# The last routing of a layer in two halves, behind given products, and VectorE in emission order in one step

## The chip, the cores and the metric

One core of one Trainium2 chip runs the whole kernel. The metric is the device time of one execution in microseconds. A profiled execution has a span as well, from its first to its last instruction.

## What is computed

An attention with decay (no softmax), then two layers of experts. Cut to what matters:

```
scores = q k^T / 8;  x = (scores * decay) v            # 4 x 8 heads, 576 x 64  ->  2304 tokens x 512
# layer 1: capacity 576 per expert
e = argmax(x w_gate);  g = softmax(x w_gate)[e]
x = g * (relu(x w1[e]) w2[e])                           # 512 -> 1024 -> 512, 8 experts
# layer 2: only tokens with x . w_skip > 0, no capacity
e = argmax(x w_gate2); g = softmax(x w_gate2)[e]
out = x + g * (relu(x w1b[e]) w2b[e])                   # skipped tokens: out = x
```

## The kernel before

The kernel is one program in a language whose planner decides the order of instructions on each engine. It places them by their order of emission and its own estimate of when their inputs are ready; a block may ask that some engines keep the order of emission (`manual_schedule`). The experts run under such a block for GpSimd (`Pool`) alone. So TensorE's, VectorE's and ScalarE's orders are the planner's, and what is emitted later can be placed earlier when it seems ready.

**Layers, steps and f.** Each layer is run as nine steps (`NST`; `pos` in the code), each with a batch of up to `CAPS[layer][pos]` tokens of one expert. In layer 2 step 0 has 240 columns, step 1 has 324 and step 2 has 240. A step runs over f = 0 to 7, blocks of 128 of the 1024 hidden units (`Layer.run`, L800). For each f there is a first product h (`s1`, L712, its matmuls in L727 or L732 to L734) and a second product y (`s2`, L740, in L755 to L757, L763 or L766 to L768). Where a step has more than 192 columns, the weights and inputs are split into a high and a low part, and each product takes three matmuls. ScalarE makes the high half `hi` (L673) and VectorE subtracts for the low half `lo` (L674), one unit (two f) ahead; h gives `hh` on ScalarE (L737) and `hl` on VectorE (L738). Step 0 of layer 2 is one of the steps in which y has tokens on its rows (`token_major`, L770); there h is emitted one f further ahead.

**Hand-over from step to step.** While a step runs, the rows of the next are gathered by an indirect transfer on GpSimd (`gather`, L683 and L838; its index is `fx` for the first steps and `gix` for the others), transposed on TensorE (`transposes`, L704: `x_1T` is that of step 1), and written as `x_1h` by ScalarE (L705) and `x_1l` by VectorE (L707). At the end of a step of layer 1, `post1` (L874) computes layer 2's logits for its tokens (`M`, `Mt`, `L`), transposes the result back to rows (`yr`, L797), writes it to memory for layer 2 and to the output, and routes the tokens: `Router.add` (L386).

**Routing.** `Router.add` is a generator that stops at its `yield`s. It takes the largest logit (`mx`, `oh`), the softmax's probability (`gt`, L331: a subtraction on GpSimd, an exponential on ScalarE, the rest on VectorE), counts per expert (`cum`, `C`), then on TensorE the ranks (`R`, L418 and L419), from them on VectorE the slot of every token (`lo`, `hi`, `A`, `k3`), products with what is to be stored per slot (`vv`, L458, and `B`, L460: token numbers and the gate in two parts), and a matmul `I` (L466) that is added to the table `inv` (L468). In names, `s8` is the routing after the last step of layer 1 and `r3` the last routing before layer 1. After the last routing `order` (L515; `fc` is its count on TensorE) sorts the experts by count, `by_order` (L530; `w` and `invp`, L538 and L540) brings a table's values into that order, `int_idx` (L590) makes the gather's index and `scatter_idx` (L579; `sif`, `six`) that of the output. `leave` (L545; names `lv2...`) and `left_out` (L959) count the tokens that found no place, for a fallback at the end.

**Where it stands before.** In layer 1's first step the routing `r3` goes on in hooks behind f = 0 and 2, and order, gates and indices follow behind f = 4 (L942). The last routing `s8` runs through to `I` in `post1`, in front of layer 2's first step, with `order` between its parts; then come `by_order([0])` and the gather's index, and in step 0 of layer 2 the gates behind f = 1 (`gates2`). The gather of step 1 is emitted at f = 0, its transposes at f = 6. `leave2` is emitted behind step 1; as its inputs are ready long before, the planner can place it earlier.

Of the kernel before, what the change touches and what calls it, by code (L numbers as in the profile page):

```python
# [11 lines left out]
F32R = mybir.dt.float32r  # L12
# [11 lines left out]
KT = 3  # L24
# [7 lines left out]
NST = 9  # L32
# [297 lines left out]

def softmax_top(g, L, T, t_, oh):  # L331

    nc = g.nc
    v_ = nc.vector
    b = [128, T, 8]
    l8 = L[:, :, 0:8]
    mx = t_("mx", [128, T])
    v_.tensor_reduce(out=mx, in_=l8, op=ALU.max, axis=AX.X)
    first_max(g, oh, l8, mx, t_("e8", b), t_("mn", [128, T]), T)
# [27 lines left out]
class Router:  # L367
# [15 lines left out]
    def ohf(g_, t0, T):  # L383
        return g_.oh[:, t0:t0 + T].bitcast(F32)

    def add(g_, t0, T, L, vals, name, late=False, mid=False):  # L386
        g, lay, nv = g_.g, g_.lay, g_.nv
        nc = g.nc
        v_ = nc.vector
# [4 lines left out]
        b = [128, T, 8]  # L394
        oh, ohf = g_.oh[:, t0:t0 + T], g_.ohf(t0, T)
        if lay == 1:
            gt = softmax_top(g, L, T, t_, oh)
            cm = None
        else:
            o1 = t_("o1", b)  # L400
            cm = t_("cm", [128, T])
            v_.tensor_single_scalar(cm, L[:, :, 8], 0.0, op=ALU.is_gt)
            gt = softmax_top(g, L, T, t_, o1)
            v_.tensor_mul(oh, o1, cm[:, :, None].to_broadcast(b))
        if late:
            s8, sh = t_("s8", b), t_("shf", [128, T])
            v_.tensor_mul(s8, ohf, g_.shift.to_broadcast(b))
            v_.tensor_reduce(out=sh, in_=s8, op=ALU.add, axis=AX.X)
# [40 lines left out]
                                in1=g.k128[:, None, :].to_broadcast([128, T, KT]), op0=ALU.mult, op1=ALU.is_equal)  # L449
        vt = t_("vt", [128, T, nv], F32R)  # L450
        vtf = vt.bitcast(F32)
        for i, x in enumerate(vals):
            nc.gpsimd.tensor_copy(vt[:, :, i], x)
        v_.tensor_copy(vt[:, :, nv - 2], gt)
        v_.tensor_sub(vt[:, :, nv - 1], gt, vtf[:, :, nv - 2])
        nc.gpsimd.tensor_copy(g_.gt[:, t0:t0 + T], gt)
        vv = t_("vv", [128, T, nv, 8])
        v_.tensor_mul(vv, v[:, :, None, :].to_broadcast([128, T, nv, 8]), vtf[:, :, :, None].to_broadcast([128, T, nv, 8]))  # L458
        Bm = t_("B", [128, T, nv * 8, KT], F32R)
        v_.tensor_mul(Bm, vv.rearrange("p t i e -> p t (i e)")[:, :, :, None].to_broadcast([128, T, nv * 8, KT]),  # L460
                      k3[:, :, None, :].to_broadcast([128, T, nv * 8, KT]))
        yield cm
        I = misc(g, f"{name}I")
        w = nv * NTAU
        for t in range(T):
            nc.tensor.matmul(I[:, 0:w], A[:, t, :], Bm[:, t].rearrange("p a k -> p (a k)"), start=(t == 0), stop=(t == T - 1))  # L466
        inv = g_.inv.rearrange("p i e k -> p (i e k)")
        v_.tensor_add(inv, inv, I[:, 0:w])  # L468

    def counts(g_, name):  # L470
        g = g_.g
# [125 lines left out]
def tokens_out(g, b):  # L597

    nc = g.nc
    n0 = 9 * (b // 2) + (4 if b % 2 else 0)  # L600
    T = 5 if b % 2 else 4
    s = K()

    def logits():
        s.l4 = g.rt1.tile([128, 640], F32, tag="l4", name=f"l4_{b}", bufs=1)
        logits4(g, g.xT[b], g.wg1, [512] if T == 4 else [320, 320], s.l4, f"L4_{b}_")

    def choose():
        L = g.rt1.tile([128, T, NL], F32, tag="L1", name=f"L1_{b}")
        token_logits(g, s.l4, T, L, f"Lt{b}_")  # L610
        s.gen = g.r1.add(n0, T, L, [g.tid1[:, n0:n0 + T]], f"r{b}", late=b > 1, mid=b == 1)
# [65 lines left out]
class Layer:  # L677
# [62 lines left out]
    def s2(self, pos, f):  # L740
# [7 lines left out]
        if self.token_major(pos):  # L748
            for k in range(TILES[2][pos]):
                n = min(128, C - 128 * k)  # L750
                y, ks = s.y[k][0:n], slice(128 * k, 128 * k + n)
                if C <= F32_MAX:
                    nc.tensor.matmul(y, s.hh[f][:, ks], w.r2[:, f % 2], start=a, stop=o)
                else:
                    nc.tensor.matmul(y, s.hh[f][:, ks], w.hi2[:, f % 2], start=a, stop=False)  # L755
                    nc.tensor.matmul(y, s.hh[f][:, ks], w.lo2[:, f % 2], start=False, stop=False)  # L756
                    nc.tensor.matmul(y, s.hl[f][:, ks], w.hi2[:, f % 2], start=False, stop=o)  # L757
            return
        for d in range(4):
            dc = slice(128 * d, 128 * d + 128)  # L760
            y = s.y[d][:, 0:C]
            if C <= F32_MAX:
                nc.tensor.matmul(y, w.r2[:, f % 2, dc], s.hh[f], start=a, stop=o)  # L763
            else:
                wh, wl = w.hi2[:, f % 2, dc], w.lo2[:, f % 2, dc]
                nc.tensor.matmul(y, wh, s.hh[f], start=a, stop=False)  # L766
                nc.tensor.matmul(y, wh, s.hl[f], start=False, stop=False)  # L767
                nc.tensor.matmul(y, wl, s.hh[f], start=False, stop=o)  # L768

    def token_major(self, pos):  # L770

# [26 lines left out]
        return n, ps  # L798

    def run(self, hooks, inner={}):  # L800
        g, lay = self.g, self.lay
        base = 4 * NST * (lay - 1)
        for pos in range(NST):
            for f in range(8):
                u = base + 4 * pos + f // 2
                if f % 2 == 0:
# [13 lines left out]
                for i in range(f + 1, f + 2 + self.token_major(pos)):  # L820
                    if i < 8:
                        self.s1(pos, i)
                    elif nx is not None:
                        nx.s1(np_, i - 8)
                self.s2(pos, f)
                if (pos, f) in inner:
                    inner[pos, f]()
            self.evac(pos)
            self.post(pos)
            if pos in hooks:  # L830
                hooks[pos]()


def gather_rows(g, src, idx, C, name, lim=None):
# [18 lines left out]
def moe(g):  # L853
# [20 lines left out]
    def post1(pos):  # L874
# [11 lines left out]
        for k in range(T):  # L886
# [6 lines left out]
        for i, cm in enumerate(r2.add(t0, T, L, [g.slot[:, t0:t0 + T], sl(r1.invp, pos, 0)], f"s{pos}", late=pos == NST - 1)):  # L893
            if i == 0 and pos == NST - 1:
                r2.order()
# [13 lines left out]
    def post2(pos):  # L909
        s = l2.st[pos]  # L910
        for k in range(TILES[2][pos]):
            n, ps = l2.rows(pos, k)
            o = g.rt.tile([128, 512], F32, tag="xr", name=f"o{pos}_{k}", bufs=6)
            v_.scalar_tensor_tensor(out=o[0:n], in0=ps[0:n], scalar=col(r2.gate, 2, pos, k, n), in1=s.rows[k][0:n], op0=ALU.mult, op1=ALU.add)  # L914
            scatter(g, col(g.si2, 2, pos, k, n), o[0:n])

    idx20 = []
# [28 lines left out]


def keep_gates(g):
# [321 lines left out]
```

## Time and profile before

| | us |
|---|---|
| median of 3 runs | 584.06 (583.22 to 586.92) |
| profiled execution | 584.51 |
| its span | 582.6 |
| TensorE busy in the span | 550.9 |
| VectorE busy | 309.7 |
| ScalarE busy | 226.3 |
| GpSimd busy | 144.8 |

Attention lasts up to about 113 us, layer 1 up to about 374, layer 2 to the end. The busy time of TensorE is that of pipelined matmuls: neighbours overlap, and the distance of two starts is what one costs. The mean granted clock of TensorE in the span is 0.982 of full speed.

### The profile page before, as it was taken

The numbers are of one execution on the slowest core, as the hardware profiler recorded it, in microseconds if no ns is written. First come the engines' busy times: TensorE is split into PE (matmuls) and PEld (weight loads), VectorE is DVE, ScalarE is ACT, GpSimd is POOL, SyncE is SP. The second block draws the span as 40 slices with busy tenths as digits, with TensorE's granted clock in tenths as the row PEclk, the third lists the DMA queues.
The fourth block names the chain that finished last, engine by engine and source line by source line (L and its number), as shares of the span: only waits on it lengthen the run. The fifth ranks groups of instructions, "written<-read, shape, count | busy, mean of one in ns | idle before, by whom it ended". The sixth has DMA issues, their size and how long they took to land.

```text
span 582.6 us, 12184 instructions
## 1 busy us (share of the span) xinstructions
PE 550.9 (95%) x4545; PEld 513.8 (88%) x4545; DVE 309.7 (53%) x926; ACT 226.3 (39%) x457; POOL 144.8 (25%) x192
## 2 busy tenths in 40 slices
PE   5999989999899999999999999879999999999991
PEld 5989879788899999999999999768998999999980
DVE  4767889445365756767676767695556201110110
ACT  2343444413444545455455555534443222112110
POOL 4355362012221140405040304050204112210110
PEclk7899999999999999999999999989999999999997
DMA  8869786187875474655465556367646378788860
GB/s 193 188 177 252 200 252 241 42 270 224 285 258 195 155 244 156 206 176 187 162 215 154 187 169 206 123 199 232 220 129 204 131 247 257 224 278 262 259 210 9
DMA packets 116085, 116.20 MB, mean 199 GB/s; under 512 B 47654, under 2 KB 88870, under 8 KB 116018
## 3 DMA queue, kind: packets, MB, share of 16 engines
q1 hardware_dynamic: 104432, 90.12, 50.8%
q0 software_dynamic: 6320, 15.74, 8.4%
q10 hardware_dynamic: 5266, 9.48, 4.4%
q8 instruction: 38, 0.62, 0.4%
q14 instruction: 29, 0.24, 0.1%
HBM read 101.11 MB, written 17.92 MB: 204 GB/s over the span
## 4 chain that ended last, share of the span: by engine, by line
PE 81%; DVE 8%; DMA 5%; SPq 1%; issue 1%; POOL 1%; ACT 1%; POOLq 0%; DVEq 0%
PE h L727 10%; PE y L763 9%; PE h L732 6%; PE h L734 6%; PE h L733 6%; PE y L767 6%; PE y L768 5%; PE y L766 5%; PE S L187 3%; PE O L229 3%; PE O L223 2%; PE yr L797 2%; PE y L755 1%; PE Tk L170 1%; PE y L756 1%; PE y L757 1%
## 5 line engine op out<-in xcount | busy, mean ns | idle before, releaser
L674 DVE TENSOR_TENSOR lo<-r,hi 128x1024 fp32r<-128x1024 f32 x80 | 97.9, 1224 | 65.2 <-ACT hi L673 63.3
L673 ACT CAST hi<-r 128x1024 fp32r<-128x1024 f32 x80 | 83.9, 1049 | 66.2 <-PE y L767 28.3
L767 PE MATMUL y<-hl,hi 128*128 128x316 f32 (+7 forms) x256 | 76.4, 300 | 0.9 <-DVE hl L738 0.8
L768 PE MATMUL y<-hh,lo 128*128 128x316 f32 (+7 forms) x256 | 75.9, 298 | 0.0
L766 PE MATMUL y<-hh,hi 128*128 128x316 f32 (+7 forms) x256 | 73.3, 298 | 0.0
L763 PE MATMUL y<-hh,r 128*128 128x168 f32 (+3 forms) x448 | 71.6, 302 | 1.6 <-ACT hh L729 1.6
L763 PEld LDWEIGHTS y<-hh,r 128*128 128x128 f32 x448 | 64.6, 190 | 2.0 <-ACT hh L729 1.8
L737 ACT ACTIVATE hh<-h 128x240 fp32r<-128x240 f32 (+8 forms) x80 | 32.1, 401 | 71.9 <-PE h L734 70.1
L785 DVE COPY yt<-y 128x168 f32<-128x168 f32 (+11 forms) x30 | 11.8, 395 | 89.0 <-ACT yt L787 64.4
L729 ACT ACTIVATE hh<-h 128x168 f32<-128x168 f32 (+4 forms) x64 | 19.3, 302 | 95.7 <-PE h L727 95.4
L845 POOL DMA_INDIRECT out<-o,six x18 | 19.2, 1065 | 144.7 <-DVE o L914 142.6
L738 DVE SCALAR_TENSOR_TENSOR hl<-h,hh 128x240 fp32r<-128x240 f32 (+8 forms) x80 | 35.4, 443 | 31.6 <-ACT hh L737 31.6
L767 PEld LDWEIGHTS y<-hl,hi 128*128 128x128 f32 x256 | 48.2, 188 | 2.1 <-DVE hl L738 1.9
L768 PEld LDWEIGHTS y<-hh,lo 128*128 128x128 f32 x256 | 48.2, 188 | 0.0
L766 PEld LDWEIGHTS y<-hh,hi 128*128 128x128 f32 x256 | 47.1, 188 | 0.1
L845 POOL DMA_INDIRECT out<-x2r,si x24 | 27.8, 1158 | 10.4 <-issue 6.0
L190 DVE TENSOR_TENSOR P<-S,tab 128x512 f32<-128x512 f32 (+1 forms) x40 | 23.7, 631 | 11.2 <-PE S L187 10.9
L838 POOL DMA_INDIRECT g<-xd,gix x20 | 23.9, 1194 | 9.4 <-issue 5.8
L154 POOL TENSOR_TENSOR vh<-v,tab 128x512 f32<-128x512 f32 x15 | 16.2, 1082 | 26.3 <-PE O L229 17.2
L207 DVE TENSOR_TENSOR st<-st,kv 64x64 f32<-64x64 f32 x96 | 20.9, 218 | 3.0
L797 PE MATMUL yr<-ident,yt 128*128 128x128 f32 (+11 forms) x148 | 21.9, 280 | 0.5 <-DVE o L914 0.5
L187 PE MATMUL S<-qT,kT 64*128 64x128 f32 x288 | 22.4, 295 | 0.0
(757 smaller groups left out, 1288.4 us busy)
## 6 DMA issues: line engine op xcount, KB each, us to landing
r<-w1a SPq DMA_DIRECT2D x36, 512.0 KB, 4.8
r<-w2a SPq DMA_DIRECT2D x36, 512.0 KB, 4.0
r<-w1b SPq DMA_DIRECT2D x36, 512.0 KB, 5.5
r<-w2b SPq DMA_DIRECT2D x36, 512.0 KB, 4.0
xd<-xr ACTq DMA_DIRECT2D x18, 256.0 KB, 3.9
k<-k SPq DMA_DIRECT2D x32, 128.0 KB, 3.3
q<-q SPq DMA_DIRECT2D x16, 256.0 KB, 3.8
v<-v SPq DMA_DIRECT2D x32, 128.0 KB, 4.1
```

Of the source, the lines that this page charges most:

```text
L187: nc.tensor.matmul(S[hh][:, c], s.kT[hp, cs], s.qT[hp, cs], start=True, stop=True)
L673: nc.scalar.copy(hi, raw)
L674: nc.vector.tensor_sub(lo, raw, hi.bitcast(F32))
L727: nc.tensor.matmul(ps, w.r1[:, c, fc], s.xh[:, c, 0:C], start=(c == 0), stop=(c == 3))
L732: nc.tensor.matmul(ps, w.hi1[:, c, fc], s.xh[:, c, 0:C], start=(c == 0), stop=False)
L733: nc.tensor.matmul(ps, w.hi1[:, c, fc], s.xl[:, c, 0:C], start=False, stop=False)
L738: nc.vector.scalar_tensor_tensor(out=s.hl[f], in0=ps, scalar=0.0, in1=s.hh[f].bitcast(F32), op0=ALU.max, op1=ALU.subtract)
L763: nc.tensor.matmul(y, w.r2[:, f % 2, dc], s.hh[f], start=a, stop=o)
L766: nc.tensor.matmul(y, wh, s.hh[f], start=a, stop=False)
L767: nc.tensor.matmul(y, wh, s.hl[f], start=False, stop=False)
L768: nc.tensor.matmul(y, wl, s.hh[f], start=False, stop=o)
L845: r = g.nc.gpsimd.indirect_dma_start(out=g.oa["out"][:, :], out_offset=IndirectOffsetOnAxis(ap=idx, axis=0), in_=rows, in_offset=None, bou ...
```

## The change

Only the order of work changes, and which engine does one subtraction. In the last routing of each layer (`last`) `Router.add` is cut into more parts. First come ranks, slots and the product for the token numbers, then their `I`; later come the softmax's probability (its subtraction now on VectorE), the product for the two gate values and a second `I`. Hooks place the parts behind given f of the next layer's first step, and each hook runs in `issue_after(mm)`: TensorE's instructions in it stay behind the last y matmul of that f. In that step the gather for step 1 is emitted at f = 3 in both layers, and its transposes and step 1's first h at f = 7. Step 0 of layer 2 is emitted in a block that keeps VectorE in order of emission; what is emitted outside it may still be placed among its instructions. The left-over count is held behind the last row product of step 1 on VectorE.

```diff
 def softmax_top(g, L, T, t_, oh):
+    return probability(g, L, T, t_, top(g, L, T, t_, oh))
...
+def probability(g, L, T, t_, mx, last=False):
...
-    nc.gpsimd.tensor_sub(sh, l8, mx[:, :, None].to_broadcast(b))
+    (v_ if last else nc.gpsimd).tensor_sub(sh, l8, mx[:, :, None].to_broadcast(b))
...
+        def gates():
+            v_.tensor_copy(vt[:, :, nv - 2], gt)
+            v_.tensor_sub(vt[:, :, nv - 1], gt, vtf[:, :, nv - 2])
+            nc.gpsimd.tensor_copy(g_.gt[:, t0:t0 + T], gt)
...
+        spread(0, nv - 2)
         yield cm
+        place(0, nv - 2)
+        yield cm
+        gt = probability(g, L, T, t_, mx, True)
+        gates()
+        spread(nv - 2, nv)
+        yield cm
+        place(nv - 2, nv)
...
         for pos in range(NST):
+            with ExitStack() as ctx:
+                if (self.lay, pos) == (2, 0):
+                    ctx.enter_context(self.g.tc.manual_schedule(engines={mybir.EngineType.Pool, mybir.EngineType.DVE}))
+                self.step(pos, inner)
+            self.post(pos)
...
-                    if f == (3 if (lay, pos) == (1, 0) else 0) and (nx is not self or pos == 0):
+                    if f == (3 if pos == 0 else 0) and (nx is not self or pos == 0):
                         nx.gather(np_)
...
-                        if f == 6:
+                        if f == (7 if pos == 0 else 6):
                             nx.transposes(np_)
...
-                    elif nx is not None:
+                    elif nx is not None and (pos or f == 7):
                         nx.s1(np_, i - 8)
...
+        gen = r2.add(t0, T, L, [g.slot[:, t0:t0 + T], sl(r1.invp, pos, 0)], f"s{pos}", late=last, last=last)
+        cm = next(gen)
+        if last:
+            g.step2 = lambda: next(gen, None)
...
+    def behind(fn):
+        def run(mm):
+            with g.tc.issue_after(mm):
+                fn()
+        return run
+
+    def order1():
+        r1.order()
+        r1.by_order([0])
+        g.gi1 = r1.int_idx(0)
+
     def gates1():
-        r1.order()
-        r1.by_order([0, 1, 2])
-        g.gi1 = r1.int_idx(0)
+        g.step3()
+        r1.by_order([1, 2])
         g.sf1, _ = r1.scatter_idx(0)
+    def ranks2():
+        g.step2()
+        r2.order()
+
+    def idx2():
+        g.step2()
+        r2.by_order([0])
+        g.gi2 = r2.int_idx(0)
+
+    def softmax2():
+        g.step2()
+
     def gates2():
+        g.step2()
         r2.by_order([1, 2, 3])
         _, g.si2 = r2.scatter_idx(1)
 
     def leave2():
-        r2.leave()
-        left_out(g)
+        with g.tc.issue_after(g.row):
+            r2.leave()
+            left_out(g)
...
-    l1.run({1: r1.leave, NST - 3: r2.pick_first, NST - 2: early2}, {(0, 0): g.step3, (0, 2): idx1, (0, 4): gates1})
-    r2.by_order([0])
-    g.gi2 = r2.int_idx(0)
-    l2.run({1: leave2}, {(0, 1): gates2})
+    l1.run({1: r1.leave, NST - 3: r2.pick_first, NST - 2: early2}, {(0, 0): behind(g.step3), (0, 2): behind(idx1), (0, 4): behind(order1), (0, 5): behind(g.step3), (0, 6): behind(gates1)})
+    l2.run({1: leave2}, {(0, 0): behind(ranks2), (0, 2): behind(idx2), (0, 4): behind(softmax2), (0, 5): behind(gates2)})
```

## Rows read from the trace of the kernel before

**Rows 1.** The page: busy us of TensorE, its share, instructions

```profile
PE 550.9 (95%) x4545; PEld 513.8 (88%) x4545; DVE 309.7 (53%) x926; ACT 226.3 (39%) x457; POOL 144.8 (25%) x192
```

**Rows 2.** TensorE's waits, 350 to 425 us: line <- releaser: total us, times, longest

```profile
PE s8I L466 <- DVE s8B L460: 3.0, 1, 3.0
PE fc L473 <- DVE C L414: 1.3, 1, 1.3
```

**Rows 3.** TensorE's waits, 100 to 150 us

```profile
PE x_1T L704 <- DMA g<-xd,fx: 1.7, 1, 1.7
```

**Rows 4.** Stretches: length, PE, PEld, DVE, ACT, POOL busy, PEclk, DMA share, GB/s

```profile
377.75:380.40 2.65, 1.41 (x12) 1.44 (x13) 2.07 (x17) 0.95 (x3) 0.00 (x0) 1.00 0.56 204
380.40:384.10 3.70, 0.71 (x5) 0.52 (x4) 3.70 (x20) 0.85 (x2) 2.19 (x3) 0.94 0.15 33
384.10:387.60 3.50, 3.50 (x14) 3.07 (x14) 3.33 (x16) 0.37 (x1) 1.12 (x2) 0.57 1.00 336
387.60:409.20 21.60, 21.60 (x140) 19.04 (x140) 13.76 (x27) 10.36 (x17) 6.04 (x5) 1.00 0.72 232
```

**Rows 5.** Timeline of layer 1's first step: start, duration (us), engine, line, operation

```profile
131.37 0.55 PE L704 MATMUL x_1T<-ident,g 128*128 128x128 f32 x3 [1.72 <-DMA g<-xd,fx]
...
133.44 1.30 PE L763 MATMUL y<-hh,r 128*128 128x168 f32 x8
...
134.58 1.30 PE L727 MATMUL h<-x_1h,r 128*128 128x168 f32 x8
```

**Rows 6.** Timeline of TensorE at the handover to layer 2

```profile
376.10 1.20 PE L797 MATMUL yr<-ident,yt 128*128 128x128 f32 x8
...
385.53 0.64 PE L755 MATMUL y<-hi,hh 128*128 128x512 f32 x1
...
387.64 0.27 PE L732 MATMUL h<-x_0h,hi 128*128 128x240 f32 x1
...
388.98 0.40 PE L755 MATMUL y<-hi,hh 128*128 128x512 f32 x1
...
390.37 0.27 PE L732 MATMUL h<-x_0h,hi 128*128 128x240 f32 x1
...
409.19 0.31 PE L766 MATMUL y<-hh,hi 128*128 128x324 f32 x1
```

**Rows 7.** Timeline of VectorE, the same stretch

```profile
378.35 0.34 DVE L564 TENSOR_REDUCE lv2cm<-oh 128x24 f32<-128x192 f32 x1
...
379.50 0.17 DVE L422 TENSOR_TENSOR s8r<-oh,s8R 128x16 f32<-128x16 f32 x1
...
388.03 0.42 DVE L538 TENSOR_TENSOR w<-inv,ord2PO 128x192 f32<-128x192 f32 x1
388.36 0.18 DVE L965 TENSOR_REDUCE lfr<-lv2left 128x1 f32<-128x24 f32 x1
...
388.88 0.18 DVE L543 TENSOR_TENSOR sgate<-invp 128x24 f32<-128x24 f32 x1
...
389.52 0.18 DVE L587 CAST six<-sif 128x24 int32<-128x24 f32 x1
390.15 1.23 DVE L674 TENSOR_TENSOR lo<-r,hi 128x1024 fp32r<-128x1024 f32 x1 [0.45 <-ACT hi L673]
391.29 0.40 DVE L738 SCALAR_TENSOR_TENSOR hl<-h,hh 128x240 fp32r<-128x240 f32 x1
391.66 1.23 DVE L674 TENSOR_TENSOR lo<-r,hi 128x1024 fp32r<-128x1024 f32 x1
...
403.74 0.89 DVE L707 TENSOR_TENSOR x_1l<-x_1T,x_1h 128x324 fp32r<-128x324 f32 x2
```

**Rows 8.** GpSimd's timeline; last, issues 370 to 420 us: count, median us to landing

```profile
386.44 1.01 POOL L838 DMA_INDIRECT g<-x2d,gix  x1 [2.23 <-DVE gix L593]
...
389.04 0.95 POOL L838 DMA_INDIRECT g<-x2d,gix  x1 [0.30 <-issue]
...
g<-x2d,gix POOLq DMA_INDIRECT x7, 6.1
```

More of the change, by code (lines that the diff above doesn't have):

```diff
@@ L331, in softmax_top, with top @@
 def softmax_top(g, L, T, t_, oh):
+    return probability(g, L, T, t_, top(g, L, T, t_, oh))
+def top(g, L, T, t_, oh):
+    l8 = L[:, :, 0:8]
+    mx = t_("mx", [128, T])
+    g.nc.vector.tensor_reduce(out=mx, in_=l8, op=ALU.max, axis=AX.X)
+    first_max(g, oh, l8, mx, t_("e8", [128, T, 8]), t_("mn", [128, T]), T)
+    return mx
+def probability(g, L, T, t_, mx, last=False):
     nc = g.nc
@@ L384, in ohf, with add @@
         return g_.oh[:, t0:t0 + T].bitcast(F32)
-    def add(g_, t0, T, L, vals, name, late=False, mid=False):
+    def add(g_, t0, T, L, vals, name, late=False, mid=False, last=False):
         g, lay, nv = g_.g, g_.lay, g_.nv
@@ L396, in add @@
         if lay == 1:
-            gt = softmax_top(g, L, T, t_, oh)
+            mx = top(g, L, T, t_, oh)
             cm = None
@@ L402, in add @@
             v_.tensor_single_scalar(cm, L[:, :, 8], 0.0, op=ALU.is_gt)
-            gt = softmax_top(g, L, T, t_, o1)
+            mx = top(g, L, T, t_, o1)
             v_.tensor_mul(oh, o1, cm[:, :, None].to_broadcast(b))
+        if not last:
+            gt = probability(g, L, T, t_, mx)
         if late:
@@ L451, in add, with spread @@
         vtf = vt.bitcast(F32)
+        vv = t_("vv", [128, T, nv, 8])
+        Bm = t_("B", [128, T, nv * 8, KT], F32R)
+        def gates():
+            v_.tensor_copy(vt[:, :, nv - 2], gt)
+            v_.tensor_sub(vt[:, :, nv - 1], gt, vtf[:, :, nv - 2])
+            nc.gpsimd.tensor_copy(g_.gt[:, t0:t0 + T], gt)
+        def spread(i0, i1):
+            n = i1 - i0
+            v_.tensor_mul(vv[:, :, i0:i1], v[:, :, None, :].to_broadcast([128, T, n, 8]), vtf[:, :, i0:i1, None].to_broadcast([128, T, n, 8]))
+            v_.tensor_mul(Bm[:, :, 8 * i0:8 * i1], vv[:, :, i0:i1].rearrange("p t i e -> p t (i e)")[:, :, :, None].to_broadcast([128, T, 8 * n, KT]),
+                          k3[:, :, None, :].to_broadcast([128, T, 8 * n, KT]))
@@ L452, in add, with place @@
+        def place(i0, i1):
+            I = misc(g, f"{name}I{i0}")
+            w = (i1 - i0) * NTAU
+            for t in range(T):
+                nc.tensor.matmul(I[:, 0:w], A[:, t, :], Bm[:, t, 8 * i0:8 * i1].rearrange("p a k -> p (a k)"), start=(t == 0), stop=(t == T - 1))
+            inv = g_.inv[:, i0:i1].rearrange("p i e k -> p (i e k)")
+            v_.tensor_add(inv, inv, I[:, 0:w])
         for i, x in enumerate(vals):
             nc.gpsimd.tensor_copy(vt[:, :, i], x)
-        v_.tensor_copy(vt[:, :, nv - 2], gt)
@@ L455, in add @@
[L455 to L461, printed above, removed]
@@ L462, in add @@
-        yield cm
[L463 to L468, printed above, removed]
+        if not last:
+            gates()
+            spread(0, nv)
+            yield cm
+            place(0, nv)
+            return
+        spread(0, nv - 2)
+        yield cm
@@ L470, in counts @@
+        place(0, nv - 2)
+        yield cm
+        gt = probability(g, L, T, t_, mx, True)
+        gates()
+        spread(nv - 2, nv)
+        yield cm
+        place(nv - 2, nv)
     def counts(g_, name):
@@ L610, in choose @@
         token_logits(g, s.l4, T, L, f"Lt{b}_")
-        s.gen = g.r1.add(n0, T, L, [g.tid1[:, n0:n0 + T]], f"r{b}", late=b > 1, mid=b == 1)
+        s.gen = g.r1.add(n0, T, L, [g.tid1[:, n0:n0 + T]], f"r{b}", late=b > 1, mid=b == 1, last=b == 3)
         next(s.gen)
@@ L752, in s2 @@
                 if C <= F32_MAX:
-                    nc.tensor.matmul(y, s.hh[f][:, ks], w.r2[:, f % 2], start=a, stop=o)
+                    self.mm = nc.tensor.matmul(y, s.hh[f][:, ks], w.r2[:, f % 2], start=a, stop=o).ins
                 else:
@@ L756, in s2 @@
                     nc.tensor.matmul(y, s.hh[f][:, ks], w.lo2[:, f % 2], start=False, stop=False)
-                    nc.tensor.matmul(y, s.hl[f][:, ks], w.hi2[:, f % 2], start=False, stop=o)
+                    self.mm = nc.tensor.matmul(y, s.hl[f][:, ks], w.hi2[:, f % 2], start=False, stop=o).ins
             return
@@ L762, in s2 @@
             if C <= F32_MAX:
-                nc.tensor.matmul(y, w.r2[:, f % 2, dc], s.hh[f], start=a, stop=o)
+                self.mm = nc.tensor.matmul(y, w.r2[:, f % 2, dc], s.hh[f], start=a, stop=o).ins
             else:
@@ L767, in s2 @@
                 nc.tensor.matmul(y, wh, s.hl[f], start=False, stop=False)
-                nc.tensor.matmul(y, wl, s.hh[f], start=False, stop=o)
+                self.mm = nc.tensor.matmul(y, wl, s.hh[f], start=False, stop=o).ins
     def token_major(self, pos):
@@ L800, in run, with step @@
     def run(self, hooks, inner={}):
-        g, lay = self.g, self.lay
-        base = 4 * NST * (lay - 1)
         for pos in range(NST):
+            with ExitStack() as ctx:
[3 more added lines that the diff above has]
+            self.post(pos)
+            if pos in hooks:
+                hooks[pos]()
+    def step(self, pos, inner):
+            g, lay = self.g, self.lay
+            base = 4 * NST * (lay - 1)
             for f in range(8):
@@ L826, in run @@
                 if (pos, f) in inner:
-                    inner[pos, f]()
+                    inner[pos, f](self.mm)
             self.evac(pos)
-            self.post(pos)
-            if pos in hooks:
-                hooks[pos]()
 def gather_rows(g, src, idx, C, name, lim=None):
@@ L892, in post1 @@
             xs.append((n, xr))
-        for i, cm in enumerate(r2.add(t0, T, L, [g.slot[:, t0:t0 + T], sl(r1.invp, pos, 0)], f"s{pos}", late=pos == NST - 1)):
-            if i == 0 and pos == NST - 1:
-                r2.order()
+        last = pos == NST - 1
+        gen = r2.add(t0, T, L, [g.slot[:, t0:t0 + T], sl(r1.invp, pos, 0)], f"s{pos}", late=last, last=last)
+        cm = next(gen)
+        if last:
+            g.step2 = lambda: next(gen, None)
+        else:
+            for _ in gen:
+                pass
         f = g.rt.tile([128, KT], F32, tag="sf", name=f"sf{pos}")
@@ L913, in post2 @@
             o = g.rt.tile([128, 512], F32, tag="xr", name=f"o{pos}_{k}", bufs=6)
-            v_.scalar_tensor_tensor(out=o[0:n], in0=ps[0:n], scalar=col(r2.gate, 2, pos, k, n), in1=s.rows[k][0:n], op0=ALU.mult, op1=ALU.add)
+            g.row = v_.scalar_tensor_tensor(out=o[0:n], in0=ps[0:n], scalar=col(r2.gate, 2, pos, k, n), in1=s.rows[k][0:n], op0=ALU.mult, op1=ALU.add).ins
             scatter(g, col(g.si2, 2, pos, k, n), o[0:n])
```

3 lines of the change are left out of this document (removed).

## The prediction

> **What bounds the kernel now.** The first view is the busy time of the engines: TensorE is busy for 95% of the span [rows 1], so a change can only win what TensorE loses, and what matters is where that is. The second view is therefore TensorE's waits, stretch by stretch. Where layer 1 hands over to layer 2 there are two: 3.0 us at the last routing's matmul `s8I` for the VectorE product `s8B`, and 1.3 us at the count `fc` for VectorE's `C` [rows 2]. In layer 1's first step there is one of 1.7 us, the transposes `x_1T` for a gather [rows 3]. The third view, busy time and granted clock by stretch, shows what the first two waits really cost: TensorE works 1.41 of 2.65 us and 0.71 of 3.70 us, and then 3.5 us pass at a granted clock of 0.57, which is close to the lower of its two levels, 1.2 GHz [rows 4]. The row of a y matmul lasts 0.64 us there (385.53) and 0.40 later (388.98) [rows 6]. After 387.6 TensorE is never idle up to 409.2 [rows 4]. So the loss sits in two places, and the change works on both.
>
> **What TensorE could gain at the handover.** I count the work from the transposes `yr` (376.10, done about 377.05 [rows 6]) to the first y matmul of step 1 of layer 2 (409.19 [rows 6]). Twelve h matmuls of step 0 take 1.34 us (387.64 to 388.98), six y matmuls 1.39 (388.98 to 390.37) [rows 6]. Still to do at 377.05: 20 h matmuls (2.2), y of f=0 (1.4), ranks and count (0.3, an estimate), h of f=3 to 7 (6.7), y of f=1 to 7 (9.7), 12 transposes `x_1T` (1.3, at 0.11 each like the h matmuls), the `I` matmuls (0.6), and 24 h matmuls of step 1 at 0.15 (3.6; its tiles are 324 columns against 240). That is 25.8 us, so 402.9. TensorE is there at 409.2: 6.3 us is the most that this place can give.
>
> **Layer 1's first step.** The transposes `x_1T` are emitted at f=7 instead of 6. Then h of f=7 and y of f=6 run first, 1.14 us per eight matmuls (133.44 to 134.58 [rows 5]), 2.3 us together. The gather that they wait for lets them go on at 131.37 [rows 5]; its index is made at the same place as before, so its landing does not move. The wait of 1.7 us is covered. The gates, which now come at f=5 and 6, are needed only after y of f=7, some 2 us after I expect them. I take 1.7; bounds 0.5 (the copies of `x_1T` are waited for instead) and 1.7.
>
> **The handover, part by part.** Three edits free VectorE. The left-over count, 13 instructions from `lv2cm` at 378.35 to `lfr` at 388.36 [rows 7], goes behind step 1: about 3 us of VectorE in the worst stretch. The product `s8B` is halved, and the softmax leaves the stretch. And the rank matmuls `s8R` and the count `fc` go behind y of f=0, so TensorE no longer stands at 377.75. The price: TensorE reaches `s8R` at 377.05 + 2.2 + 1.4 + 0.3 = 381.0, while VectorE read it at 379.50 before [rows 7]. Everything that follows on VectorE starts 1.5 us later.
>
> **VectorE in program order.** This is the edit that I cost in full, because what waits on VectorE now holds up all that was emitted behind it: weights' low halves (`lo`), which h and y of later f need, and the products `hl`. A `lo` holds VectorE for 1.14 us and an `hl` for 0.37 (starts at 390.15, 391.29, 391.66 [rows 7]). A chain of dependent small instructions goes at 0.21 (`sgate` to `six`, three steps in 0.64 [rows 7]); two chains mixed go closer. From 381.05:
> ranks (10) and order (8) at 0.21, plus 0.2 for the wide `A`: 4.0, with `hl` of f=3 done at 385.5. `lo` of the next unit 386.65 and 387.8. TensorE meanwhile has h of f=3, y of f=1 and 2 and `I`, to 385.4, then y of f=3: hardly a wait, because given products lie in front. `hl` of f=4 must wait for its h, which had to wait for `lo`: VectorE idles 1.0 and ends at 389.25. The index: inverse add 0.28, one `w` with its reduction 0.85 (388.03 to 388.88 [rows 7]), cast 0.2: the gather of step 1 is issued about 390.8, against 386.44 before [rows 8]. It is three tiles, 1.3 apart (386.44 to 389.04 [rows 8]), and lands 6.1 later (median [rows 8]): 399.5. Then `hl` of f=5, two `lo` (393.25), 1.0 idle again, `hl` of f=6 (394.7), the softmax and the second product (8 at 0.21, and 0.5 for the exponential on ScalarE: 396.9), `hl` of f=7 (397.3), which TensorE's last y needs: it is done at 398.7. Behind that on VectorE stand the gates (0.28 + 3 x 0.85 + 4 x 0.21 = 3.7: 401.1), two `lo` (403.4) and only then the four subtractions `x_1l` at 0.45 (0.89 for two [rows 7]): 405.3. Step 1's h matmuls need these. So TensorE has nothing but `x_1T` from 398.7 to about 404, and ends h of f=0 and 1 of step 1 at about 407.5: 1.7 us ahead of 409.2.
>
> That idle stretch looks like the one before the half clock [rows 4]. Half clock for about 3 us costs 1.5 more, and the gain would be 0.2. I take 0.8 between them, for the transposes still break the idle time. Bounds: +6.3 (TensorE never waits) and -2.7 (five handovers of 0.6 more from TensorE to VectorE, and the half clock).
>
> A rule of the Trainium skill bears on the price of program order (VectorE: DVE Perf Modes, The DRAIN you can't avoid): a VectorE instruction does not start before the pipe of the one before it is empty, with or without a wait between them. The rows don't bear that out fully: `lfr` starts at 388.36 while `w`, from 388.03, lasts 0.42 [rows 7]. By the rule mixing two chains wins nothing, so program order costs nothing; that is rival four.
>
> **Smaller parts.** The subtraction for the softmax moves from GpSimd to VectorE: one step of 0.21, counted above; GpSimd's scatters of x2r, which stood behind it and the gate copy, go earlier, and nothing waits for them. The gather of step 2 stands on GpSimd behind the gate copy: about 397, landing about 405, needed only during step 1. SP reads the order of experts after the order is made, at about 385, and starts the weights of step 1 then; VectorE converts them only after 401. The left-over count lies behind step 1's rows, where VectorE converts for step 2: about 4 us of small instructions among waits of the same size. I take a loss of 0.3; bounds 0 and 2.
>
> **The sum.** The profiled execution took 584.51 (span 582.6): 584.5 - 1.7 - 0.8 + 0.3 = 582.3. The median of the runs is 0.45 below that execution, so 581.9.
>
> **The rivals.**
> One, TensorE never waits: VectorE's idle times are filled and `x_1l` comes in time. For it: TensorE's demand is 25.8 us, VectorE's from 381.05 only about 22 without its waits. Against: these 22 us alone end at 403. 584.5 - 6.3 - 1.7 = 576.5, as a median 576.1; it covers 576 to 580 as waits remain.
> Two, slower: VectorE's fixed order holds `x_1l` back so long that the wait moves into step 1. Place: the gates and two `lo` ahead of `x_1l`. Price: 2.7 at the handover, 2 at the count, half of the layer 1 gain: 584.5 + 4.7 - 0.9 = 588.3, as a median 587.9. It decides if the last `x_1l` ends after about 408. For it: VectorE is full from 381 on. Against: each price is at its bound.
> Three, the stall only changes place: half clock in front of step 1, the transposes of layer 1 wait for their copies: 584.5 - 0.2 - 0.5 + 0.3 = 584.1, as a median 583.7.
> Four, program order is free: 26 small instructions at 0.17 instead of 0.21 save 1.0: 581.3, as a median 580.9. The steps from `sgate` to `six` speak against it.
>
> **How the numbers follow.** Likeliest 0.45 (581.9, its own range 580 to 584), one 0.20, two 0.13, three 0.15, four 0.07. A measurement here tells about 1% from no change, 5.8 us. Faster by more than that is below 578.2: the better part of rival one, 0.13. Slower is above 589.9: the far end of rival two, 0.05. The rest, 0.82, is within 1%. The range leaves out half of rival one below and half of rival two above: 578.0 to 586.5.
>
> **What would show it.** Right: no wait at `s8I` or `fc`; `x_1T` of layer 1 without its 1.7; VectorE busy almost throughout from 381 to 405; TensorE idle just before `x_1l`, in front of step 1 of layer 2, and a clock below 1 behind it; the gather of step 1 issued some 4 us later. Wrong: TensorE busy throughout that stretch (rival one); a wait for `I` in spite of the products in front; waits of TensorE after step 1 for `lo` or `hl`, which I have only at 0.3.

## The result: slower by 0.7%, most of it by a term sized at 0.3 us

The changed kernel takes 588.81 us (median of 11 runs, 587.0 to 590.4); the kernel before takes 584.31 beside it (11 runs). The ratio is 1.0074, with a 95% interval of 1.0057 to 1.0091. The forecast was 581.9 with a range up to 586.5. The time went up by 4.5 us, where a small gain was forecast.

The profiled execution took 589.9 us (span 587.8, before 582.6). On the page TensorE's row, which answers to [rows 1], says little: 3.7 us more busy time, with only seven more matmul rows (the second `r3I` and the second `s8I`). The stretches below show that most of this is time at a lower clock; the rest of the longer span is idle time.

```profile
PE 554.6 (94%) x4552; PEld 516.9 (88%) x4552; DVE 313.4 (53%) x934; ACT 226.8 (39%) x457; POOL 143.5 (24%) x190
```

TensorE's waits in the changed kernel (line <- releaser: total us, times, longest), from 350 to 425 us, which answers to [rows 2], and from 425 to 470:

```profile
PE h L767 <- DVE lo L707: 2.7, 2, 1.9
PE x_1T L737 <- DVE x_1l L740: 2.2, 1, 2.2
...
PE lfp L1033 <- DVE lfr L1031: 3.9, 1, 3.9
PE yr L830 <- DVE o L958: 0.5, 1, 0.5
```

The waits at `s8I`, `fc` and layer 1's `x_1T` [rows 2, 3] are gone, as the change wants it. Three others stand there now: h waits for weights' low halves, the last transposes `x_1T` wait for an `x_1l` that is late, and the left-over count's matmul `lfp` waits 3.9 us for its input. That one is the largest, and it lies in a stretch where the kernel before waits only 0.5 us. The stretches of the changed kernel show what follows each wait (columns as in [rows 4]):

```profile
381.60:383.60 2.00, 0.11 (x2) 0.08 (x1) 1.96 (x5) 0.43 (x1) 0.00 (x0) 1.00 0.00 0
383.60:387.30 3.70, 3.70 (x15) 3.26 (x16) 1.41 (x2) 0.37 (x1) 0.00 (x0) 0.54 0.88 293
...
399.30:403.40 4.10, 1.87 (x9) 1.12 (x8) 3.93 (x10) 1.48 (x3) 0.00 (x0) 1.00 0.23 65
403.40:407.40 4.00, 4.00 (x19) 4.00 (x20) 3.77 (x6) 0.86 (x2) 2.05 (x2) 0.61 0.86 311
...
440.04:443.93 3.89, 0.00 (x1) 0.03 (x1) 3.61 (x12) 0.91 (x2) 3.05 (x3) 1.00 0.60 214
443.93:449.00 5.07, 5.07 (x25) 4.41 (x26) 1.93 (x6) 0.37 (x1) 1.78 (x1) 0.66 0.75 251
```

Each time TensorE is idle for some 2 to 4 us, and after it the granted clock is 0.54, 0.61 and 0.66 for 3.7, 4.0 and 5.1 us, that is, at or near the lower of the two levels (1.2 GHz) for most of it. Had that work run at full clock, it would have taken 3.70 x 0.46 = 1.7, 4.00 x 0.39 = 1.6 and 5.07 x 0.34 = 1.7 us less (an estimate from these rows). So each of these waits cost 1.6 to 1.7 us on top of its own length.

**Where the time went.** I took three stretches out of each trace: layer 1's first step (from y of f = 0 to the first `M`), the handover (from the first `M` of layer 1's last step to the first y of layer 2's step 1, `408.91` in the changed kernel, 409.19 before [rows 6]), and the count's stretch (from the first `yr` of step 1 to the last `x_8T`). Everything behind it lasts the same to 0.1 us in the traces compared.

| kernel (one execution each, us) | layer 1's first step | handover | count's stretch | median us, ratio to the kernel before, 95% |
|---|---|---|---|---|
| before | 22.01 | 34.50 | 111.90 | 584.31 |
| changed | 20.75 | 37.26 | 117.41 | 588.81, 1.0074 (1.0057 to 1.0091) |
| e1 layer 1's edits only | 20.75 | 35.23 | 111.90 | 582.83, 0.9961 (0.9941 to 0.9982) |
| e2 count not held back | 20.75 | 39.62 | 111.90 | 587.89, 1.0049 (1.0032 to 1.0065) |
| e3 VectorE free | 20.75 | 33.74 | 118.40 | 587.54, 1.0034 (1.0010 to 1.0057) |
| e4 held count only | 22.42 | 33.68 | 118.15 | 589.66, 1.0074 (1.0048 to 1.0101) |
| e5 `lfp` later | 21.87 | 37.12 | 113.14 | 587.00, 1.0016 (0.9994 to 1.0039) |
| e6 `lfp` later, VectorE free | 21.87 | 33.98 | 113.12 | 584.60, 0.9982 (0.9964 to 0.9999) |
| e7 `lfp` later, layer 2 whole and free | 21.86 | 33.73 | 113.12 | 584.36, 0.9978 (0.9958 to 0.9998) |
| e8 e5 with the ranking later | 21.86 | 38.93 | 113.14 | 590.25, 1.0076 (1.0049 to 1.0103) |
| e9 e6 with the count at step 3 | 20.75 | 33.08 | 111.67 | 579.22, 0.9911 (0.9888 to 0.9934) |
| e10 e9 with the slots sooner | 20.75 | 30.55 | 111.66 | 577.83, 0.9886 (0.9871 to 0.9902) |
| e11 e7 with VectorE in order | 20.75 | 38.68 | 113.14 | 586.59, 1.0037 (1.0024 to 1.0050) |
| e12 e9, `lfp` placed by the planner | 20.75 | 32.13 | 112.25 | 581.15, 0.9947 (0.9926 to 0.9968) |

Ratios are against runs of the kernel before on the same chip: 584.8 for e1 to e4, 585.4 for e5 to e8, 584.3 for e9 to e11, 583.9 for e12. For the changed kernel the three stretches sum to -1.26 + 2.76 + 5.51 = +7.0 us; its span grew by 5.2, because two waits that differ from execution to execution (a y of layer 1 for `hh`, and `x_0T` for its gather) were 1.8 us shorter in this one (1.6 and 0.9 before, 0.7 and none here). The medians, 4.5 apart, hold more of that spread than one trace can show. The stretches spread too: with the same code there, the handover took 34.50 us in the kernel before and 35.23 in e1, and 32.13 to 33.98 in e3, e6, e9 and e12.

### The profile page after: what moved, and what is told of

Its sections match the earlier page's. It is cut to its first block, busy times and chain, and to the rows that moved or that the text cites. A ratio compares the mean times of both kernels' runs of the same rounds, so it can differ in the third digit from the quotient of the medians.

```text
span 587.8 us, 12204 instructions
## 1 busy us (share of the span) xinstructions
PE 554.6 (94%) x4552; PEld 516.9 (88%) x4552; DVE 313.4 (53%) x934; ACT 226.8 (39%) x457; POOL 143.5 (24%) x190
## 4 chain that ended last, share of the span: by engine, by line
PE 83%; DVE 10%; issue 2%; DMA 2%; SPq 1%; ACT 1%; ACTq 0%; POOL 0%; POOLq 0%; DVEq 0%
PE h L760 11%; PE y L796 10%; PE h L767 7%; PE h L765 7%; PE h L766 6%; PE y L800 6%; PE y L801 6%; PE y L799 5%; PE S L187 3%; PE O L229 3%; PE yr L830 2%; PE O L223 2%; PE Tk L170 1%; PE Tq L170 1%; PE y L786 1%
```

## The experiments

**e1 to e4: which part costs what.** e1 takes the change's layer 1 alone, e2 takes back the count's edit, e3 takes VectorE out of the block in program order, and e4 is the kernel before with the count's edit alone.

```diff
 e1  -l2.run({1: leave2}, {(0, 0): behind(ranks2), ..., (0, 5): behind(gates2)})
     +r2.by_order([0]); g.gi2 = r2.int_idx(0)
     +l2.run({1: leave2}, {(0, 1): gates2})        # and post1, gather, s1 of layer 2 as before
 e2  -with g.tc.issue_after(g.row):                # in leave2; the two calls stay
 e3  -manual_schedule(engines={Pool, DVE})
     +manual_schedule(engines={Pool})
 e4  +with g.tc.issue_after(g.row):                # in leave2 of the kernel before
```

> The changed kernel with layer 2 as before: only the edits in layer 1's first step are left. In the changed kernel's trace layer 1 ends 3.0 us earlier (first matmul M of the last routing at 371.65 against 374.69). Theory: this is the edits' own gain, so about 3.0 below the kernel before (ratio 0.995), and the waits x_1T (1.7) and x_0T (0.9) are gone. Rival, the prediction's term: only the 1.7 of x_1T, ratio 0.997, the rest being a shift that the planner makes for other reasons.

> The changed kernel without the hold on the left-over count (its instructions may again be placed early). Theory: the hold costs 5.5 us, 3.9 of wait at TensorE's matmul lfp and about 1.6 of half clock behind it, so 5.5 below the changed kernel, ratio to the kernel before 0.998. Rival: the count's 13 instructions return to VectorE's full stretch at the handover and cost about 3 there: ratio 1.003.

> The changed kernel with VectorE left to the planner in layer 2's first step (GpSimd still in order). Theory: the order of emission is what cost TensorE its waits for lo (2.7) and x_1l (2.2) there, so about 3 to 5 below the changed kernel, ratio to before 1.000 to 1.002. Rival: the waits come from the amount of VectorE's work and from the late start of the ranks, and the order changes little: ratio 1.007 as the changed kernel.

> The kernel before with one edit: the left-over count held behind the last row product of step 1 of layer 2. Theory: the matmul lfp again waits about 3.9 and the clock falls behind it, plus 5.5; VectorE's three freed us at the handover give back up to 2, so ratio 1.006 to 1.009. Rival: the wait at lfp needs the rest of the change; the count alone changes nothing or wins up to 2 at the handover, ratio 0.997 to 1.000.

Layer 1's edits are a gain: 1.26 us in the trace, 0.4% in the median, less than the 3.0 us that I expected. Against e4, which has layer 1 as before and ran on the same chip, the step is 22.42 - 20.75 = 1.67 us shorter. The held count is a loss by itself: in e4, on the kernel before, the same `lfp` wait of 3.9 us appears and the count's stretch grows by 6.25 us, while the handover falls by only 0.8, about what executions of the same code differ by (34.50 and 35.23 above):

```profile
442.68 0.56 PE L968 MATMUL lfp<-lfr,tab 128*128 128x2 f32 x2 [3.88 <-DVE lfr L966]
```

In e2 that loss is gone, but twelve instructions of the count (`lv2G` to `lfr`, 383.36 to 386.61 us in its trace) stand in VectorE's order ahead of the low halves, and the handover is 2.4 us longer than in the changed kernel. Its waits:

```profile
PE h L767 <- DVE lo L707: 5.6, 2, 4.8
PE x_1T L737 <- DVE x_1l L740: 2.2, 1, 2.2
```

With VectorE free (e3) the waits for `lo` and `x_1l` are gone and the handover falls by 3.5 us, to 33.74. The ratio, 1.0034, is above the 1.000 to 1.002 that I expected; the count's stretch is 1.0 us longer in this trace. What is left at the handover is a wait for the gather:

```profile
PE x_1T L737 <- DMA g<-x2d,gix: 2.4, 2, 1.9
PE y L790 <- DVE hl L771: 0.7, 1, 0.7
```

**e5 to e7: the count's matmul.** `lfp` is one matmul of two columns. The planner put it behind the third of the twelve h matmuls of hidden block 2 of step 2, and TensorE takes its queue in order. The timelines of the changed kernel, VectorE first (start, us, engine, line, operation, what it waited for):

```profile
439.87 0.16 DVE L1030 TENSOR_REDUCE lfr<-lv1left 128x1 f32<-128x18 f32 x1
439.94 1.21 DVE L707 TENSOR_TENSOR lo<-r,hi 128x1024 fp32r<-128x1024 f32 x1
...
443.61 0.18 DVE L1031 TENSOR_REDUCE lfr<-lv2left 128x1 f32<-128x24 f32 x1
...
443.93 0.35 PE L1033 MATMUL lfp<-lfr,tab 128*128 128x2 f32 x2 [3.89 <-DVE lfr L1031]
```

The chain that ends in `lfr` begins behind the last output row at 439.30, with a low half of 1.21 us inside, and ends at 443.79. TensorE has stood at `lfp` since 440.04, with nine matmuls of h, which read the same tiles as the three ahead of it, and everything later behind it. e5 moves nothing but that matmul and its three readers:

```diff
 def left_out(g): ...
-    ps = misc(g, "lfp"); nc.tensor.matmul(ps[:, 0:2], g.ones, r, ...)   # and flag
+    g.lfr = r                                     # the rest into count_left(g)
-l2.run({1: leave2}, {..., (0, 5): behind(gates2)})
+l2.run({1: leave2}, {..., (0, 5): behind(gates2), (2, 3): behind(count_left)})
```

e6 is e5 with e3's edit, e7 is e5's edit on e1's layer 2, with the count held.

> The changed kernel, with one matmul moved: the sum of the left-over count (lfp, 128x2) and the three small VectorE instructions that read it stand behind TensorE's y of hidden block 3 of layer 2's step 2, instead of where the planner put it, inside the matmuls of hidden block 2. VectorE's work of the count stays held back as in the changed kernel. Theory A (the place of lfp in TensorE's queue is the loss: TensorE waits 3.9 us there and then runs 1.6 us longer at half clock): the stretch from the end of step 1 to the last transposes goes from 117.4 back to 111.9 us, and the time to 588.8 - 5.5 = 583.3 us. Theory B (VectorE's held-back load is the loss, wherever lfp stands): the stretch stays above 115 us, with waits of h or y for VectorE there, time 587 us or more.

> As e5_lfp_later, and VectorE not in program order in layer 2's first step (the planner orders it; only GpSimd keeps program order). Theory A: layer 1 keeps its gain of 1.3 us, the handover stands at 33.7 us (0.8 below the 34.5 of the kernel before), the count's stretch at 111.9: 584.3 - 1.3 - 0.8 = 582.2 us, below both kernels. Theory B (VectorE's held-back load): the count's stretch stays at 117 to 118 us and the time at 587 us.

> Layer 1 as in the changed kernel; layer 2's first step as in the kernel before (all of the ranks, slots and gates at once, VectorE ordered by the planner); the left-over count held behind step 1's last output row, its matmul behind y of hidden block 3 of step 2. It tells what splitting layer 2's routing is worth against e6. If the split (slots first, gates later) is worth nothing by itself: handover 33.7, time 582.2 us as in e6. If the split is what brings the 0.8 us at the handover: handover 34.5, time 583.0.

The wait at `lfp` goes in all three, and the stretch falls from 117.4 to 113.1 us: 4.3 of the 5.5. The rest, 1.2 us, stayed, where theory A wanted all of it back: y waits 1.1 us for an `hl` that stands behind the count's chain on VectorE (e5, 412 to 470 us):

```profile
PE y L790 <- DVE hl L771: 1.1, 1, 1.1
```

So the place was the larger part and VectorE's load the smaller. The medians came out 2 to 4 us above what I expected: on this chip layer 1's first step took 21.87 instead of 20.75, with 0.6 us at `x_1T` that the trace puts down to no releaser, and the kernel before is 1.1 us slower there than beside the changed kernel. e6 and e7 have handovers of 33.98 and 33.73, so cutting layer 2's routing in two shows no gain in this pair; the same handover code as e6's took 33.74, 33.08 and 32.13 us in e3, e9 and e12, so at best it is 1.6 us.

**e8 and e11: program order.**

```diff
 e8  in ranks2: -r2.order()
     in step, (layer 2, step 0, f = 2): +convert_unit(g, u + 1); +r2.order()    # ahead of load_unit
 e11 in e7:     +manual_schedule(engines={Pool, DVE})
```

> As e5_lfp_later (VectorE in program order), and in layer 2's first step the ranking of the experts (fc, key, PO, ord) stands behind the low halves of weight unit 2 in VectorE's program order instead of ahead of them. Theory C (the program order costs because the ranking and its wait for TensorE stand ahead of the low halves: h waits 1.9 us for lo and the clock falls to half): the wait of h for lo goes, the handover falls from 37.3 to about 35 us, time 583.3 - 2.2 = 581.1 us. Theory D (VectorE is simply full in program order, or the gather, now later, is what comes last): the handover stays at 37 us or more, with the wait at x_1T for x_1l or for the gather longer than 2.2 us, time 583.3 us or more.

> As e7_old2_lfp_later (layer 2's routing whole, as in the kernel before; the count's matmul placed late), with VectorE in program order in layer 2's first step. It is the fourth corner beside e5 (split, in order: handover 37.1), e6 (split, free: 34.0) and e7 (whole, free: 33.7). If program order costs by itself: handover 36 us or more, time 587 us or more. If it costs only together with the split routing, whose ranks then stand ahead of the low halves: handover 34 us, time as e7.

e8's time is the one that theory D expects, but by neither theory's mechanism. The first wait for `lo` did shrink, from 1.75 us in e5 to 0.68, and the clock stayed full there, as theory C has it. But a wait of 4.17 us took its place, through two queues that I had not followed. Rows of e8 on VectorE, SP, ScalarE and TensorE:

```profile
388.48 0.17 DVE L561 CAST ord2ord<-ord2of 128x8 int32<-128x8 f32 x1
...
389.47 0.38 SPq L689 DMA_DIRECT2D r<-w1b  x1
...
393.00 1.04 ACT L706 CAST hi<-r 128x1024 fp32r<-128x1024 f32 x1 [5.40 <-DMA r<-w1b]
...
394.35 0.41 DVE L771 SCALAR_TENSOR_TENSOR hl<-h,hh 128x240 fp32r<-128x240 f32 x1 [4.23 <-ACT hi L706]
394.67 2.35 DVE L707 TENSOR_TENSOR lo<-r,hi 128x1024 fp32r<-128x1024 f32 x2
...
395.94 0.57 PE L767 MATMUL h<-x_0h,lo 128*128 128x240 f32 x1 [4.17 <-DVE lo L707]
```

SP issues the weights of step 1 0.8 us after the order of experts is made (in the changed kernel that is at 382.85, behind 381.86). ScalarE's queue has their high half (`hi`, 393.00) ahead of `hh` of block 5; `hl` of block 5 waits for that, and the low halves of unit 39 stand behind that `hl` in VectorE's program order. The ranking is thus needed soon for a second reason, the weights. e11 gives the fourth corner: with the routing whole, program order costs 38.68 - 33.73 = 5.0 us (e11 and e7 are from different chips); with it cut in two, e5 and e6 give 37.12 - 33.98 = 3.1 on one chip. e11's median, 586.6, is just under the 587 that I had set for a cost of program order by itself, and its handover is well above the 36. So program order costs by itself.

Why it does is in VectorE's rows. In the changed kernel the ranking stands ahead of the low halves that h of block 4 needs:

```profile
381.86 0.17 DVE L561 CAST ord2ord<-ord2of 128x8 int32<-128x8 f32 x1
381.94 0.40 DVE L771 SCALAR_TENSOR_TENSOR hl<-h,hh 128x240 fp32r<-128x240 f32 x1
382.26 2.35 DVE L707 TENSOR_TENSOR lo<-r,hi 128x1024 fp32r<-128x1024 f32 x2
...
400.50 0.18 DVE L620 CAST six<-sif 128x24 int32<-128x24 f32 x1
400.59 2.35 DVE L707 TENSOR_TENSOR lo<-r,hi 128x1024 fp32r<-128x1024 f32 x2
402.86 0.89 DVE L740 TENSOR_TENSOR x_1l<-x_1T,x_1h 128x324 fp32r<-128x324 f32 x2
```

In e6, free, the planner puts that `lo` in the time in which VectorE waits for the ranks, and the ranking after it:

```profile
381.40 1.22 DVE L707 TENSOR_TENSOR lo<-r,hi 128x1024 fp32r<-128x1024 f32 x1
...
383.17 0.16 DVE L433 TENSOR_TENSOR s8r<-oh,s8R 128x16 f32<-128x16 f32 x1
...
385.38 0.17 DVE L561 CAST ord2ord<-ord2of 128x8 int32<-128x8 f32 x1
```

**e9, e10, e12: a version that beats both.** e9 moves the count on to step 3, from where on no step needs low halves, and `lfp` to step 4. e12 is e9 with `lfp` placed by the planner again. e10 is e9 with `s8I` put behind h of block 4 instead of y of block 2, and the low half of unit 39 put behind the gather's index.

```diff
 e9  -l2.run({1: leave2}, {..., (2, 3): behind(count_left)})
     +l2.run({3: leave2}, {..., (4, 3): behind(count_left)})
 e10 +(0, 2): idx2 behind the last h matmul of block 4, emitted ahead of y of block 2
     +with g.tc.issue_after(g.gixm): convert_unit(g, u + 1)   # f = 4; gixm: the cast to gix
 e12  in leave2: left_out(g); +count_left(g)                  # no (4, 3)
```

> As e6_free_lfp_later, with the left-over count two steps later: its VectorE work behind the last output row of step 3 instead of step 1, its matmul behind y of hidden block 3 of step 4. In e6 1.2 us of the count's 5.5 was left, as a wait of y for hl (1.1 us). If that rest is VectorE's load around step 2, where it also makes low halves (8.15 us busy of 9.00 us in 436 to 445 us), it goes in the later steps, where VectorE is busy 2 us of 10: the stretch from yr of step 1 to the last x_8T falls from 113.1 to 111.9 us, and the time to 1.2 us under e6, 0.4% under the kernel before. If the rest is something else that moved with e6 (the place of other matmuls), the stretch stays at 113.1 and the time at e6's.

> As e9_count_at_3, but the count's matmul lfp is again placed by the planner. VectorE has nothing else to do at that point, so the run tells the place of lfp in TensorE's queue from VectorE's load. The planner puts lfp 15 matmuls of 0.146 us (2.2 us) behind the last yr of step 3, at 480.7 us on e9's clock, while the chain of 14 VectorE instructions behind the last output row ends there at 483.2. If the place is the loss, TensorE waits 2.5 us at lfp for lfr, though VectorE is otherwise idle; with what the clock then costs the time is 2.5 to 4.5 us above e9. If it was VectorE's load at step 2 that made lfp late (the low half of 1.21 us stood inside the chain), TensorE waits under 0.5 us and the time is e9's.

> As e9_count_at_3, and in layer 2's first step the slots of step 1 come sooner: the slots' matmul s8I stands behind the matmuls of hidden block 4 instead of behind y of hidden block 2, and the low half of weight unit 39 stands on VectorE behind the gather's index gix instead of ahead of it. In e6 gix is at 389.43 us and x_1T waits 2.6 us for the gathers that read it. If the gather's start is what sets that wait: gix about 1.5 us sooner, the wait at x_1T 1.1 us or less, the handover 34.0 down to about 32.5 us, the time 1.5 us under e9. If the gathers are held by the queue or by the weights' transfers beside them: the wait stays above 2 us and the time at e9's. If the low half of unit 39 then comes late: a wait of h for lo takes its place.

In e9 the last 1.2 us of the count are gone (111.67). Against the kernel before it won 0.7% more than e6, not 0.2%: besides 1.45 us at the count its execution has 1.1 less in layer 1's first step (20.75 again) and 0.9 less at the handover, where the code is e6's. e12 was to tell place from load, and I had reckoned the place wrongly: the profile counts each of these matmuls twice, so the 15 in front of `lfp` last 4.5 us, not 2.2. There the planner's place fits:

```profile
482.38 0.18 DVE L1032 TENSOR_REDUCE lfr<-lv2left 128x1 f32<-128x24 f32 x1
...
482.71 0.35 PE L1042 MATMUL lfp<-lfr,tab 128*128 128x2 f32 x2 [0.29 <-DVE lfr L1032]
```

So the planner does not misplace such a matmul always. It did at step 2, by 3.9 us, with VectorE busy there (3.61 of 3.89 us), and hardly at step 4. But e12 does not tell place from load, for both changed: behind the last output row TensorE reached `lfp` after 0.7 us at step 2 (439.38 to 440.04) and after 3.2 at step 4 (479.26 to 482.42), and the chain took 4.4 us there and 3.3 here. The later place is the larger part in e12 as well (2.5 of 3.6 us); a quiet VectorE alone was not tried. (The spans of e9 and e12, 579.1 and 579.0 us, are alike; their medians are from different chips.) Why its estimate was so far off at step 2 stays open: the low half inside the chain is 1.2 of the 3.9.

e10 is 1.1% faster than the kernel before, and by the two ratios 1.9% faster than the changed one. Its waits between 366 and 412 us, and the whole handover in two stretches:

```profile
PE x_0T L737 <- DMA g<-x2d,fx: 1.2, 1, 1.2
PE x_1T L737 <- DMA g<-x2d,gix: 1.0, 1, 1.0
PE y L790 <- DVE hl L771: 0.7, 1, 0.7
```

```profile
373.49:400.00 26.51, 24.81 (x165) 20.85 (x166) 20.56 (x68) 12.25 (x22) 9.73 (x10) 1.00 0.57 196
400.00:404.04 4.04, 4.04 (x28) 3.88 (x27) 2.95 (x10) 1.89 (x4) 1.01 (x1) 1.00 0.99 346
```

The index is 14.2 us behind the first `M` (387.71), against 15.5 in e6; the wait at `x_1T` falls from 2.6 to 1.0, and the granted clock is 1.00 throughout. Against e12, whose handover ran at full clock too, that is 1.6 us, the 1.5 expected; against e9 it is 2.5, as e9 ran from 398 to 402 us at 0.56 and 0.59. These are single executions: on the chip that ran both, the medians of e9 and e10 are 1.4 us apart and their intervals overlap. e10's two edits were not run apart.

## Why the prediction was wrong

**Layer 1, term 1.7: right in mechanism, 1.26 in size.** The wait [rows 3] is gone, and `x_1T` runs behind the second `r3I`, 0.6 us of TensorE (131.79 to 132.38) that the term left out:

```profile
131.79 0.75 PE L481 MATMUL r3I<-r3B,r3A 128*128 128x48 f32 x5
132.38 0.44 PE L737 MATMUL x_1T<-ident,g 128*128 128x128 f32 x2
```

The size is not sharp: e4 and e1, on one chip, give 1.67. In e5 to e8 the step is only 0.15 us shorter than in the kernel before, with a pause at `x_1T` that no row explains; but no run shows what the kernel before takes there, for the chip of its trace is not on record.

**The count, term 0.3 (bounds 0 and 2): this is the step that failed.** It measured 5.5 us. The term took the count for "small instructions among waits of the same size" on VectorE. It left out that the last of them feeds a matmul, so that the count also has a place in TensorE's queue. The edit holds VectorE's chain back behind the last output row, but it leaves that place to the planner. What was queued behind the waiting instruction was never named, though it was nine matmuls of h and all that follows them. Length of the wait 3.9, half clock after it 1.7, together 5.6.

**The handover, term -0.8 (bounds -6.3 and +2.7): +2.8.** Put on the old clock by the `yr` of the handover (376.10 before [rows 6], 373.05 after, so 3.05 are added to times of the changed kernel), the timetable for VectorE held at first: `s8R` 381.0 against 380.8, the low halves 385.5 against 385.3. The gather was issued at 392.2 instead of 390.8, and `x_1l` began at 405.9 instead of 403.4. The sentence that failed is "hardly a wait, because given products lie in front". They do not lie in front: in this step h is emitted one f further ahead, so h of block 4 comes ahead of y of block 2, and the planner kept TensorE to that but for two matmuls of y. The third matmul of that h needs `lo`:

```profile
377.72 0.17 PE L429 MATMUL s8R<-oh,utr 128*128 128x16 f32 x1
...
380.79 0.27 PE L765 MATMUL h<-x_0h,hi 128*128 128x240 f32 x1
...
381.25 0.39 PE L789 MATMUL y<-lo,hh 128*128 128x512 f32 x1
383.53 0.38 PE L767 MATMUL h<-x_0h,lo 128*128 128x240 f32 x1 [1.89 <-DVE lo L707]
...
385.59 0.64 PE L790 MATMUL y<-hi,hl 128*128 128x512 f32 x1
...
403.40 0.55 PE L737 MATMUL x_1T<-ident,g 128*128 128x128 f32 x3 [2.23 <-DVE x_1l L740]
...
408.91 0.32 PE L799 MATMUL y<-hh,hi 128*128 128x324 f32 x1
```

Two waits for `lo` of 2.7 us and the half clock of 1.7 behind the first make 4.4, and the forecast end of step 1's h (407.5) and the real one (408.91 + 3.05 = 412.0) are 4.5 apart. The stall in front of step 1, which the prediction did name, came out about even: the forecast end holds some 4 us of idle time at full clock there (398.7 to 404, less 1.3 of transposes), and the trace has 2.2 us and then a clock of 0.61, worth 1.6. But "the transposes still break the idle time" held for six of the twelve only: the others waited themselves, for `x_1l`.

**The rivals.** Two, "slower", came nearest: it had 2.7 at the handover and 2 at the count, for 587.9. It was given 0.13, because each price stood at its bound. Its mechanism, `x_1l` behind the gates and two `lo`, is the second of the two stalls; the first, and the matmul of the count, were in no rival. One ("TensorE never waits") is what e10 comes close to: the handover gives 3.95 of the 6.3 us. Four (program order is free) fell: e5 against e6 and e11 against e7 price it at 3.1 and 5.0 us. The price lies in what stands behind the waiting instructions, not in the small steps themselves. The rule that the prediction set beside this rival (the Trainium skill, VectorE: DVE Perf Modes, The DRAIN you can't avoid) has an exception in the same paragraph: a next instruction that is not held starts earlier. The row of `lfr`, which starts 0.09 us before `w` ends [rows 7], goes with the exception.

**The signs.** No wait at `s8I` or `fc`, no 1.7 at layer 1's `x_1T`, TensorE idle before `x_1l`, the gather later (5.7 us on the old clock, 4 forecast): these came. VectorE "busy almost throughout from 381 to 405" did not: on the old clock it was busy 16.9 of these 24.0 us, and idle between times, mostly for `hh`. Of the lines that were to prove it wrong, "waits of TensorE after step 1 for `lo` or `hl`, which I have only at 0.3" came in another form: the wait was for `lfr`, which no line named. It stood beside the smallest term of the sum.

## What to carry to other kernels

Holding a chain back on one engine delays every instruction that reads its result, and here TensorE took its queue in order (3.9 us at `lfp`, nine matmuls of h behind it): name the reader in the other engine's queue and all that stands behind it, and give it a later place together with the chain. Program order on an engine is worth what stands behind its waiting instructions; here the planner's own order was 3 to 5 us better. The gather's index and the order of experts, which the weight loads read, have separate readers, and each can set the pace: the order 3.3 us later, counted from the first `M`, brought a wait of 4.2 by way of the weights (e8 against e5), and the index 1.3 us sooner, with a low half moved behind it, shortened the handover by 1.6 to 2.5 (e10 against e12 and e9).

## What was not expected

The half clock does not follow the length of a wait alone. In the changed kernel waits of 1.9, 2.2 and 3.9 us were each followed by it, for about 1.6 us of loss. In e9 three waits of 0.51, 0.53 and 0.68 us with single transposes between were too; in e12 waits of 0.43 and 1.89 us at the same place were not:

```profile
398.00:400.00 2.00, 1.74 (x7) 1.68 (x8) 0.77 (x3) 0.86 (x2) 0.00 (x0) 0.56 1.07 377
400.00:402.00 2.00, 2.00 (x10) 1.70 (x9) 1.06 (x3) 0.15 (x1) 0.00 (x0) 0.59 1.05 371
```

```profile
398.00:400.00 2.00, 1.05 (x6) 0.78 (x7) 0.22 (x1) 0.68 (x2) 0.00 (x0) 1.00 1.07 374
400.00:402.00 2.00, 2.00 (x15) 1.86 (x15) 1.96 (x6) 0.69 (x3) 0.00 (x0) 1.00 1.04 373
```

The first two rows are of e9, the last two of e12, and TensorE had less idle time in e9. What made the difference no run here shows. And with the same edits layer 1's first step took 20.75 us on the chips of most runs and 21.87 on another, with a pause of 0.6 us at `x_1T` for which the trace shows no releaser; that stays open.
